# Polynomial sketch attention and a normalised two-layer network on one core: the same calls in another written order, with other PSUM banks

## The chip, the cores and the metric

One Trainium2 chip, one of its cores. The metric is the device time of one execution in microseconds (us), the median of several runs. The engines of a core are TensorE (PE; PEld is its weight load), VectorE (DVE), ScalarE (ACT), GpSimd (POOL) and SyncE (SP), which here only issues DMAs. Each runs its own queue in the written order and waits on semaphores of the others.

## The reference, cut to what matters

```python
def phi(x):                                   # x: (4, 4, 1088, 32), S1, S2: (8, 32)
    a = einsum('rd,bhsd->bhsr', S1, x)
    b = einsum('rd,bhsd->bhsr', S2, x)
    return einsum('bhsi,bhsj->bhsij', a, b).reshape(..., 64)
q_p, k_p = phi(q), phi(k)
kv  = einsum('bhsf,bhsd->bhfd', k_p, v);  z = sum(k_p, axis=2)
x   = einsum('bhsf,bhfd->bhsd', q_p, kv) / (einsum('bhsf,bhf->bhs', q_p, z) + 1e-6)
x   = x.transpose(0, 2, 1, 3).reshape(4, 1088, 128)      # heads side by side
xn  = (x - mean(x)) / sqrt(var(x) + 1e-6) * g_ln         # over the last axis
out = x + maximum(xn @ w_ch1, 0) @ w_ch2                 # (128, 512), (512, 128)
```

Queries, keys, values and the gain are float32; S1, S2 and both weights come as float64, and the kernel puts float32 words together from their halves. All matmuls are float32.

## The kernel before, in words

There are four batches, 0 to 3. The 1088 tokens of a batch and its four heads go through these calls; each call is a small function in the kernel, and its name is used below.

*Words of S, W1 and W2.* `w_ex`, `w_bits`, `w_mant`, `w_e2`, `w_low`, `w_add`, `w_e3` (the sign merge, L310), `w_mul` (L87 by its helper) work with integer and float operations on DVE, ACT and POOL. Index 0 is S, 1 is W1, 2 is W2. `s_heads` ends S (tile s_f), `w_mul 1` gives w1g, and `fold` multiplies it by a centring matrix with the gain, so that W1 already subtracts the mean.

*Keys.* `ld k b` brings the keys of batch b (tile kn, two buffers: batches 0 and 2 share one, 1 and 3 the other). `turn_g` and `turn_r` turn them on DVE (L419, L429), `k_feat` multiplies them by the sketch (L537, tiles of 64x32), `k_tok` turns the result (L546, tile kf), `k_prod` forms the 64 products on POOL (L87, tile kp, one buffer for all batches), `k_val` sums products with values (L587, needs all of V of its batch), `k_vcp`, `k_spr` (L602), `k_rcp` bring the sum into tile kvr. `k_sum` (L561), `k_zs`, `k_sc` (L575) and `k_sccp` make the vector for the denominators; for batch 0 `k_scr`, `gram_d`, `gram_r` do that.

*Values.* `ld_v b g` loads a quarter of V (32 partitions, 128 KB), `ld_vr` a rest of 16 KB. Each batch has a V tile of its own.

*Queries.* Batch 0 is turned by TensorE (`turn_p`, L438, copied by `turn_c`) and multiplied by `q_dir` (L621); the others are turned by DVE, then `q_feat` (L655) and `q_tok` (L664). `q_ac`, `q_den`, `q_rec`, `q_a2`, `q_prod` form denominators and products (DVE and POOL, L87, L677, L684), `q_turn` (L702, L707, L712) turns the products. `num` (L725, tiles of 32x32) multiplies them by kvr; `num_cp` and `num_r` copy the numerators into xT and xTr.

*The network.* Its rows go in chunks: c 0 to 7 are halves of the batches (512 rows, batch c // 2), 8 and 9 hold the remaining rows of two batches each. `row_turn`, `row_wr`, `row_rd` bring a chunk through DRAM into rows (tile x); `st_bn`, `st_ag`, `st_pow` give the reciprocal deviation (tile rstd). `hid z c j t0 t1` (L834) multiplies xT by a quarter j of W1 into PSUM bank z, `relu` copies it into one of two hidden buffers hT (which one goes by the chunk's place in 0, 1, 2, 3, 8, 4, 5, 6, 7, 9), `sec z c t` (L850) multiplies a block of 128 rows by W2 into bank z. `fin` (DVE), or `fin_a` (ACT) and `fin_g` together, scale by rstd and add x; `store` and `store_r` write out.

*Fillers.* `fill n w z` runs n products of ones, w columns wide, into bank z. Their results are not used.

*What sets the order.* Nothing is scheduled by a planner. The string PROGRAM (L901) lists all 498 calls; a loop behind it makes them in that order, so each engine's queue is this list restricted to its calls. A, V, G, S in a call name the engine ACT, DVE, POOL or SP. The numbers z are PSUM banks, chosen by hand: a call that writes a bank waits until the copies out of it are done. An engine stands still behind the first call that waits.

```python
    for line in PROGRAM.split(";"):
        if line.split():
            name, *args = line.split()
            ops[name](*(int(a) if a.isdigit() else a for a in args))
```

## Time and profile before

| | |
|---|---|
| median of 3 runs | 103.19 us (102.77 to 103.45) |
| the profiled execution | 103.05 us, span of its instructions 101.2 us |
| granted TensorE clock | 1.00 throughout |
| read from HBM, written | 9.84 MB, 4.33 MB |
| PE | 95.8 us busy, 1273 matmuls |
| DVE, POOL, ACT | 73.2, 57.9, 38.8 us busy |

An fp32 product shows as two matmuls, a transpose as one. A matmul's end is modelled and lies behind the start of the next one, so distances between starts are the measure of what PE spends. In the DMA rows the last number is the time from issue to landing. In the waits, "issue" stands where the profile shows no releaser.

### The profile page before, as it was taken

What the parts mean: (1) busy time and instruction counts of PE and PEld (TensorE: products, weight loads), DVE (VectorE), ACT (ScalarE), POOL (GpSimd) and SP (SyncE); (2) the same over time, 40 slices, a digit from 0 to 9 for tenths busy, and PEclk for the clock granted to TensorE, in tenths of its full rate; (3) what the DMA queues carried; (4) which work ended last, traced back from release to release, by engine and by line L of the source; (5) the groups of instructions that cost most, each with busy time, mean ns of one, the idle gap of its engine ahead of it and who ended that gap; (6) DMA issues with size and microseconds to landing.
All of it is one profiled execution on the core that took longest, in us unless ns stands there. A gap on an engine that the chain in (4) does not pass through costs nothing.

```text
span 101.2 us, 3143 instructions
## 1 busy us (share of the span) xinstructions
PE 95.8 (95%) x1273; PEld 67.2 (66%) x1273; DVE 73.2 (72%) x213; ACT 38.8 (38%) x92; POOL 57.9 (57%) x80
## 2 busy tenths in 40 slices
PE   4999999999899999999999999999999999999970
PEld 2634777667453989674559794786378966888950
DVE  5397799989697899599998455998939029833440
ACT  3460523237296311253775183065550532133000
POOL 6046998999339979947099990195193400403400
PEclk9999999999999999999999999999999999999999
DMA  2898999999179500025550055700004661200341
GB/s 32 294 361 291 269 218 216 345 279 286 41 233 305 148 15 6 0 84 161 189 158 4 6 207 187 233 1 0 0 6 176 242 197 40 104 0 6 125 170 41
DMA packets 13119, 14.37 MB, mean 142 GB/s; under 512 B 2480, under 2 KB 10160, under 8 KB 13104
## 3 DMA queue, kind: packets, MB, share of 16 engines
q1 hardware_dynamic: 12912, 14.09, 45.8%
q8 instruction: 10, 0.16, 0.7%
q10 hardware_dynamic: 192, 0.07, 0.3%
q14 instruction: 5, 0.04, 0.1%
HBM read 9.84 MB, written 4.33 MB: 140 GB/s over the span
## 4 chain that ended last, share of the span: by engine, by line
PE 94%; DVE 1%; issue 1%; ACT 1%; ACTq 1%
PE ALL L850 31%; PE ALL L834 30%; PE ALL L257 8%; PE ALL L725 7%; PE ALL L587 4%; PE ALL L537 3%; PE ALL L621 2%; PE ALL L655 2%; PE ALL L438 1%; PE ALL L561 1%; PE ALL L602 1%; PE ALL L367 1%; ACTq L894 1%; DVE ones L196 0%; PE ALL L575 0%
## 5 line engine op out<-in xcount | busy, mean ns | idle before, releaser
L850 PEld LDWEIGHTS ALL<-w,hT 128*128 128x128 f32 x272 | 32.2, 192 | 4.8 <-issue 4.0
L850 PE MATMUL ALL<-w,hT 128*128 128x128 f32 x272 | 33.7, 277 | 0.0
L834 PE MATMUL ALL<-xT,w 128*128 128x512 f32 (+1 forms) x72 | 30.7, 552 | 0.0
L842 ACT ACTIVATE hT<-ALL 128x512 f32<-128x512 f32 (+2 forms) x34 | 15.8, 486 | 16.2 <-PE ALL L834 9.3
L834 PEld LDWEIGHTS ALL<-xT,w 128*128 128x128 f32 x72 | 12.3, 190 | 8.0 <-issue 5.0
L87 POOL TENSOR_TENSOR kp<-kf 128x768 f32<-128x768 f32 (+2 forms) x9 | 17.4, 1943 | 0.0
L87 POOL TENSOR_TENSOR qp<-a,fq 128x512 f32<-128x512 f32 (+3 forms) x7 | 13.8, 1979 | 3.2 <-DVE a L87 3.0
L818 POOL TENSOR_TENSOR va<-mv,eps 128x4 f32<-128x4 f32 (+1 forms) x10 | 2.0, 200 | 15.9 <-DVE mv L813 15.9
L868 ACT ACTIVATE ob<-ALL,rstd 128x128 f32<-128x128 f32 x20 | 6.9, 370 | 10.5 <-PE ALL L850 3.8
L257 PE MATMUL ALL<-ones 128*128 128x256 f32 (+1 forms) x18 | 9.3, 642 | 1.5 <-DVE ones L196 1.5
L820 POOL TENSOR_TENSOR rstd<-va,mhalf 128x4 f32<-128x4 f32 (+1 forms) x10 | 9.2, 923 | 2.3 <-DVE ob L863 1.6
L82 ACT COPY xT<-ALL 128x256 f32<-128x256 f32 x10 | 5.8, 648 | 10.2 <-PE ALL L725 8.0
L787 DVE STREAM_TRANSPOSE xh<-ALL 128x256 f32<-128x256 f32 x16 | 6.3, 421 | 4.4 <-issue 2.7
L844 DVE TENSOR_SCALAR hT<-ALL 128x512 f32<-128x512 f32 (+2 forms) x10 | 6.0, 604 | 3.9 <-PE ALL L834 3.9
L725 PE MATMUL ALL<-qpT,kvr 32*32 32x288 f32 (+2 forms) x320 | 7.8, 364 | 0.6 <-issue 0.4
L863 DVE SCALAR_TENSOR_TENSOR ob<-ALL,rstd,x 128x128 f32<-128x128 f32 x12 | 3.7, 343 | 6.1 <-PE ALL L850 5.4
L702 DVE STREAM_TRANSPOSE qpT<-qp 128x1024 f32<-128x1024 f32 (+1 forms) x6 | 8.0, 1348 | 0.0
L807 DVE BATCH_NORM_STATS2 st<-x 128x6 f32<-128x128 f32 x32 | 6.8, 273 | 0.0
L315 POOL TENSOR_TENSOR mant<-mant,low 128x512 f32<-128x512 f32 x2 | 2.5, 1271 | 7.2 <-ACT mant L298 7.2
L725 PEld LDWEIGHTS ALL<-qpT,kvr 32*32 32x32 f32 x320 | 4.1, 103 | 3.6 <-issue 1.0
L257 PEld LDWEIGHTS ALL<-ones 128*128 128x128 f32 x18 | 4.0, 250 | 3.7 <-DVE ones L196 1.5
L664 DVE STREAM_TRANSPOSE fq<-ALL 128x576 f32<-128x576 f32 x6 | 4.3, 763 | 2.6 <-PE ALL L655 2.4
(111 smaller groups left out, 115.6 us busy)
## 6 DMA issues: line engine op xcount, KB each, us to landing
kn<-in_k_dram SPq DMA_DIRECT2D x4, 544.0 KB, 5.9
vn<-in_v_dram SPq DMA_DIRECT2D x16, 128.0 KB, 4.2
xd<-xh SPq DMA_DIRECT2D x8, 256.0 KB, 2.3
x<-xd SPq DMA_DIRECT2D x8, 256.0 KB, 3.7
out_dram<-ob SPq DMA_DIRECT2D x7, 256.0 KB, 2.4
qn<-in_q_dram SPq DMA_DIRECT2D x3, 544.0 KB, 7.0
w_raw<-in_moe_w_ch_dram SPq DMA_DIRECT2D x2, 512.0 KB, 5.7
qt<-in_q_dram SPq DMA_DIRECT2D x1, 512.0 KB, 5.3
```

Source lines behind the costliest of these rows:

```text
L87: by[eng].tensor_tensor(out=o, in0=a, in1=b, op=ALU.mult)
L257: pe.matmul(bank(z, 0, w), ones[:, 0:P], ones[:, 0:w], start=True, stop=True)
L702: dve.transpose(_ap(qpT, 0, P, 32 * u0, [[32, u1 - u0], [TW, 8], [1, 32]]), qp[:, H * F * u0 : H * F * u1])
L725: pe.matmul(bank(z[r], o, o + w)[D * h : D * h + D], kvr[b % 2][rows, DM * f + D * h : DM * f + D * h + D], qpT[rows, c : c + w], start=(f ...
L787: dve.transpose(_ap(xh[slot(c)], 0, P, 64 * n * i, [[32 * n, 2], [32, n], [1, 32]]), pair(z, P * (c % 2), [[32, n], [1, 32]]))
L807: dve.bn_stats(out=sts[slot(c)][:, 6 * t : 6 * t + 6], in_=row_ap(c, t))
L820: pool.tensor_tensor(out=rstds[slot(c)][:, 0:n], in0=vas[slot(c)][:, 0:n], in1=mhalf[:, 0:n], op=ALU.pow)
L834: pe.matmul(bank(z, 0, n), w1[:, P * j : P * (j + 1)], cols(c)[:, a : a + n], start=True, stop=True)
L842: act.activation(o, i, AF.Relu)
L844: by[eng].tensor_scalar(out=o, in0=i, scalar1=0.0, scalar2=None, op0=ALU.max)
L850: pe.matmul(bank(z, DM * t, DM * (t + 1)), h[:, 512 * j + P * t : 512 * j + P * (t + 1)], w2[:, DM * j : DM * (j + 1)], start=(j == 0), st ...
L868: act.activation(ob(c)[:, P * t : P * (t + 1)], bank(z, P * t, P * (t + 1)), AF.Copy, scale=rstds[slot(c)][:, t : t + 1])
```

## The change

The function bodies stay as they are; PROGRAM is another list. It has 498 calls again, of the same kinds: 44 `hid`, 34 `sec`, five `num`, four each of `k_feat` and `k_val`, three 512-wide and six 256-wide `fill`, the same loads and stores. Every engine gets its calls in another order, most PSUM banks differ, and some calls are on another engine: `w_mant 0` on ACT instead of DVE, `w_mul 2` and a net of one `q_a2`, two `q_ac` and one `q_prod` on POOL instead of DVE, a net of three `relu`, two `num_r` and one `num_cp` on DVE instead of ACT.

Of the list, its head:

```diff
-    ld_s A 1; c_iota; c_small; ld_s A 0; c_ones; fill 1 512 7; fill 1 256 5; fill 1 256 4; c_vpad 0;
+    ld_s A 1; c_vpad 0; c_rest; c_small; c_iota; c_pads 0; c_ones; fill 1 256 5; fill 1 512 4; ld_s
...
```

Three places carry the steps of the prediction.

First SP's queue at its start. kn_68 holds batches 0 and 2, kn_69 batches 1 and 3; qt is q of batch 0, vn_74 is V of batch 0, vn_75 V of batch 1, w_raw here is W2.

```order
 L123 DMA kn_68<-in_k_dram 128x1088
+L123 DMA kn_69<-in_k_dram 128x1088
+L146 DMA qt<-in_q_dram 128x4x256
 L155 DMA qt<-in_q_dram 64x4x32
-L146 DMA qt<-in_q_dram 128x4x256
-L123 DMA kn_69<-in_k_dram 128x1088
 L123 DMA kn_68<-in_k_dram 128x1088
-L131 DMA vn_74<-in_v_dram 32x4x256
+L165 DMA w_raw<-in_moe_w_ch_dram 128x4x128
 L137 DMA vn_74<-in_v_dram 32x4x32
-L131 DMA vn_74<-in_v_dram 32x4x256 x2
+L131 DMA vn_74<-in_v_dram 32x4x256 x3
```

Keys 1 now go out ahead of the queries of batch 0; W2 stands directly behind keys 2 and ahead of all of V 0. Before, W2 followed q 1 and parts of V 1 and V 3, ten places later. V of batches 1 to 3 follows later than before relative to the other loads: ahead of most of V 1 stand now k 3 and q 3.

Second PE's queue between the first numerators and the second part of them. kf_133 and skq are keys and sketch of batches 2 and 1, qT_99 the queries of batch 1, xT_149 is chunk 0.

```order
 L575 MATMUL ALL<-zT,s2b 128x32
+L561 MATMUL ALL<-kf_133 32x32 x9
 L725 MATMUL ALL<-qpT,kvr_138 32x128 x32
-L561 MATMUL ALL<-kf_133 32x32 x9
-L257 MATMUL ALL<-ones 128x256
-L834 MATMUL ALL<-xT_149,w_123 128x256 x2
 L655 MATMUL ALL<-qT_99,skq_103 32x288 x16
+L834 MATMUL ALL<-xT_149,w_123 128x256 x5
 L575 MATMUL ALL<-zT,s2b 128x32
-L834 MATMUL ALL<-xT_149,w_123 128x256 x4
 L725 MATMUL ALL<-qpT,kvr_138 32x160 x32
```

`k_sum 2` moved ahead of the first `num`, a fill went (to the head, ahead of `k_feat 0`), and `q_feat 1` stands ahead of all `hid`, of which five instead of six come before the second `num`. Further up, both `fold` moved from beside `k_spr 0` to between `q_dir` and `k_sum 1`, ahead of `k_val 0`.

Third POOL's queue in the middle. kp is the product of keys, qp that of queries, w_124 is W2, ac and a are denominators' terms and scaled sketches, rstd_184 and rstd_183 belong to chunks 1 and 0. Before:

```order
L87 TENSOR_TENSOR kp<-kf_134 128x1280
L87 TENSOR_TENSOR ac_101<-fq 128x16x8
L87 TENSOR_TENSOR ac_101<-fq 128x20x8
L315 TENSOR_TENSOR mant_120<-mant_120,low_121 128x512
L410 COPY skq_104<-skq_103 128x16
L87 TENSOR_TENSOR a_148<-fq,rden_146 128x128
L87 TENSOR_TENSOR qp<-a_148,fq 128x1024
L87 TENSOR_TENSOR a_148<-fq,rden_146 128x160
L87 TENSOR_TENSOR qp<-a_148,fq 128x1280
L818 TENSOR_TENSOR va_180<-mv_177,eps 128x4
L820 TENSOR_TENSOR rstd_183<-va_180,mhalf 128x4
```

And now:

```order
L87 TENSOR_TENSOR kp<-kf_134 128x1280
L87 TENSOR_TENSOR a_148<-fq,rden_146 128x160
L87 TENSOR_TENSOR a_148<-fq,rden_146 128x128
L87 TENSOR_TENSOR qp<-a_148,fq 128x1280
L87 TENSOR_TENSOR qp<-a_148,fq 128x1024
L237 MEMSET vn_76 64x4x32
L87 TENSOR_TENSOR kp<-kf_133 128x1280
L87 TENSOR_TENSOR kp<-kf_133 128x1024
L87 TENSOR_TENSOR ac_100<-fq 128x16x8
L87 TENSOR_TENSOR ac_100<-fq 128x20x8
L818 TENSOR_TENSOR va_181<-mv_178,eps 128x4
L820 TENSOR_TENSOR rstd_184<-va_181,mhalf 128x4
```

W2's addition and its product w_124 now stand above the first row shown; below it, both products of batch 2's keys come ahead of the first rstd, and chunk 1's comes ahead of chunk 0's. In ACT's queue `fin_a 4 1 0`, which needs that rstd, stands directly ahead of `num_cp A 1 1 4 8`, `k_vcp 2`, `num_cp A 1 0 4 8` and `fin_a 5 1 3`; before, the first `fin_a` of chunk 1 came behind all copies of that `num`.

On PE the groups `k_feat 3`, `k_val 1`, `q_feat 2` now follow each other, as do `num 1`, `k_sum 3`, `k_val 2`. On DVE the two operations `w_bits 1` and `w_ex 1` stand between the operations on S, `k_zs 0` behind `turn_g k 1`, and `w_e3 2` behind `q_tok 1`. At the end the last `sec` is that of chunk 9 in both lists; `fin 4 7 1` now stands between it and the last `fin`. `c_act`, a single ACT operation on one column, moved from the end of the list to the first `hid`.

## The prediction

> **What bounds the kernel now.** I read the page first: busy shares, then the chain that ended last.

> ```profile
> PE 95.8 (95%) x1273; PEld 67.2 (66%) x1273; DVE 73.2 (72%) x213; ACT 38.8 (38%) x92; POOL 57.9 (57%) x80
> PE 94%; DVE 1%; issue 1%; ACT 1%; ACTq 1%
> ```

> TensorE is busy 95% of the span and is 94% of the chain. The change removes no operation, so time can only come from places where PE waits, where it changes shape, or from the two ends. Next I read who PE waited for; these are its two longest:

> ```profile
> PE ALL L257 <- DVE ones L196: 1.5, 1, 1.5
> PE ALL L725 <- issue: 0.4, 1, 0.4
> ```

> The 1.5 is the start and stays. The ends of matmuls are modelled, so part of a wait hides behind them; the starts are measured. I therefore read PE's timeline by its starts (start, length, what), up to where the network part begins:

> ```profile
> 8.73 0.72 PE L537 MATMUL ALL<-kT,sk 64*32 64x288 f32 x16
> 9.37 1.13 PE L257 MATMUL ALL<-ones 128*128 128x512 f32 x2
> 10.43 0.38 PE L561 MATMUL ALL<-kf 128*32 128x32 f32 x18
> 12.12 1.10 PE L621 MATMUL ALL<-skd,qT 128*128 128x96 f32 x8
> 15.97 1.21 PE L587 MATMUL ALL<-kp,vn 128*32 128x64 f32 x72
> 19.37 1.44 PE L725 MATMUL ALL<-qpT,kvr 32*32 32x128 f32 x64 [0.22 <-ACT w L82]
> 21.72 1.10 PE L834 MATMUL ALL<-xT,w 128*128 128x256 f32 x4
> 22.75 0.77 PE L655 MATMUL ALL<-qT,skq 32*32 32x288 f32 x32
> 23.45 0.41 PE L575 MATMUL ALL<-zT,s2b 128*128 128x32 f32 x2
> 25.60 0.46 PE L725 MATMUL ALL<-qpT,kvr 32*32 32x160 f32 x4
> 26.42 1.14 PE L725 MATMUL ALL<-qpT,kvr 32*32 32x160 f32 x60 [0.37 <-issue]
> 27.50 4.57 PE L834 MATMUL ALL<-xT,w 128*128 128x256 f32 x12
> ```

> What a group costs is the distance to the next start. Behind 27.50 I find no further wait, only a price for changing between full tiles and tiles of 32 rows or columns. In the chain of waits three `sec` stand once between two tiled groups and once between full ones:

> ```profile
> 57.03 2.87 PE ALL L850 x24
> 79.11 2.68 PE ALL L850 x24
> ```

> Two borders cost 0.19 us, about 0.1 each.

> **Term 1, the head up to the first `hid`.** S goes through DVE, then the keys are turned, and POOL multiplies (two of the three products of batch 0 in the last row):

> ```profile
> 6.09 0.41 DVE L87 TENSOR_TENSOR s_f<-mant,ex 8x256 f32<-8x256 f32 x1
> 6.62 1.25 DVE L419 STREAM_TRANSPOSE kT<-kn 128x1024 f32<-128x1024 f32 x1
> 11.81 1.23 DVE L419 STREAM_TRANSPOSE kT<-kn 128x1024 f32<-128x1024 f32 x1
> 10.65 2.97 POOL L87 TENSOR_TENSOR kp<-kf 128x768 f32<-128x768 f32 x2
> ```

> The change puts two operations on W1's words (some 0.4 each) among those on S, where one stood before, and sends one operation on S round by ACT: s_f ends near 7.05 instead of 6.50, the turn near 8.4, the sketch near 8.55. PE has one fill more in that time, and `k_feat 0` starts at 8.7 as before. Behind it now stand two fills, one as in the row at 9.37 (1.06 to the next start, its wait included) and one half as wide (0.5): `k_sum 0` starts near 10.85 instead of 10.43. `k_zs` now stands behind the 1.23 turn of batch 1's keys and ends near 11.6; `k_scr`, the query turns and `gram_d` behind it put `q_dir 0 4` at 12.45 instead of 12.12. From `q_dir` to `k_val 0` PE took 3.85; the same groups stand there now and the two folds with them (two 256-wide matmuls, 0.9): `k_val 0` at 17.2. POOL's three products are ready near 15.3 (from 10.8, 1.5 each). `num` started 3.40 behind `k_val`; the folds (0.9) leave that stretch, the wait of 0.22 for the second one's copy goes too, `k_sum 2` (0.38) comes in: `num` at 19.85. `q_feat 1` waits for the turn of q 1 on DVE, which the order lets start near 19.8 and which takes 1.2 and a small one: 21.2. It runs 0.7, and `hid` stands behind DVE's copy of the numerators: 22.2. Before, `hid` began at 21.72 with `q_feat` (22.75 to 23.45) still to do, as good as 22.42. Term 1: **-0.2**, between -0.7 (PE free of the 0.4 that the fills hold it up) and +1.6 (V late, below).

> **Term 2, the wait inside `num 0 4 9`.** Four matmuls start at 25.60 and sixty at 26.42. The whole took 1.90; sixty took 1.08, so 64 without the hole take some 1.25. They wait for DVE's turn of the products that POOL makes last. In the new order POOL has them near 21.7, DVE has turned them by 24.4, and PE arrives at 24.6. **-0.65**; at worst 0, if DVE is later than PE by as much as now.

> **Term 3, borders.** From the first `hid` to the end the old order has nine runs of tiled groups. The new one sets `k_feat 3, k_val 1, q_feat 2` and `num 1, k_sum 3, k_val 2` side by side and does `q_feat 1` before the first `hid`: six and a half. 2.5 x 0.19 is **-0.5**, between -0.3 and -0.6.

> **Term 4, new waits.** POOL gets W2's last product, and by its order has no pause for sixteen us behind it. The product needs DVE's sign merge (last two rows, W1's and W2's):

> ```profile
> 9.08 1.26 POOL L87 TENSOR_TENSOR w1g<-mant,ex 128x512 f32<-128x512 f32 x1 [0.81 <-DVE ex L310]
> 25.23 0.93 POOL L87 TENSOR_TENSOR ac<-fq 128x128 f32<-128x128 f32 x2
> 31.89 2.29 POOL L87 TENSOR_TENSOR qp<-a,fq 128x1024 f32<-128x1024 f32 x1
> 34.67 2.40 POOL L87 TENSOR_TENSOR qp<-a,fq 128x1280 f32<-128x1280 f32 x1
> 39.11 1.95 POOL L87 TENSOR_TENSOR kp<-kf 128x1024 f32<-128x1024 f32 x1
> 38.10 1.03 POOL L820 TENSOR_TENSOR rstd<-va,mhalf 128x4 f32<-128x4 f32 x1
> 8.24 0.68 DVE L310 SCALAR_TENSOR_TENSOR ex<-w_raw,e 128x512 uint32<-128x512 uint32 x1
> 30.26 1.13 DVE L310 SCALAR_TENSOR_TENSOR ex<-w_raw,e 128x512 uint32<-128x512 uint32 x1
> ```

> The merge follows DVE's turns and a `q_tok` and ends near 26.0. From there POOL owes 1.26 (W2), 0.93 (`q_ac 1`), 2.40 (`k_prod 1 0 5`, as wide as the row at 34.67), 0.93 (`q_a2 1`), 2.40, 2.29, 2.40, 1.95 (`q_prod 1`, `k_prod 2`), 0.93 (`q_ac 2`) and 1.25 (`st_pow 1`): 16.7, with small overlaps 16.5, so `rstd` of chunk 1 comes at 42.5. `fin_a 4 1 0` on ACT waits for it, and behind it are queued two `num_cp`, `k_vcp` and `fin_a 5 1 3`, of such lengths:

> ```profile
> 42.84 0.36 ACT L868 ACTIVATE ob<-ALL,rstd 128x128 f32<-128x128 f32 x1
> 44.27 0.62 ACT L82 COPY xT<-ALL 128x256 f32<-128x256 f32 x1
> ```

> That ends near 44.8, and `hid 5 3 0`, which needs the copy and the bank, would be PE's turn at 44.5: 0.3. Two closer meetings, `hid 2 3 3` behind the relu of its bank and `num 3` behind DVE's `q_turn 4 9`, get 0.25 more as an estimate. **+0.55**, between 0 and +1.4.

> The tail stays: in both orders the last `sec` is followed by one `fin` on DVE and a store on two queues. `c_act` leaves the end of ACT's queue and costs ACT some 0.2 near 22.5, where it has room before its next relu.

> ```profile
> 97.67 0.35 DVE L863 SCALAR_TENSOR_TENSOR ob<-ALL,rstd,xr 128x128 f32<-128x128 f32 x1 [0.47 <-PE ALL L850]
> ```

> Sum: -0.2 - 0.65 - 0.5 + 0.55 = **-0.8 us**. The profiled execution took 103.05 (its span 101.2 and 1.85 around it), so 102.25 for its like. The median shown, 103.19, lies 0.14 above it, and I forecast **102.4**.

> **Rivals.** *V of batch 0 is late: slower.* W2 now goes out behind the keys of batch 2 and ahead of V of batch 0. Issue (start) and landing (last number, us from the issue) of W2, of keys 3 behind it and of the last part of V 0:

> ```profile
> 13.79 0.43 SPq L165 DMA_DIRECT2D w_raw<-in_moe_w_ch_dram  x1
> w_raw<-in_moe_w_ch_dram SPq DMA_DIRECT2D x1, 512.0 KB, 7.8
> 14.46 0.35 SPq L123 DMA_DIRECT2D kn<-in_k_dram  x1
> kn<-in_k_dram SPq DMA_DIRECT2D x1, 544.0 KB, 9.0
> 10.77 0.43 SPq L131 DMA_DIRECT2D vn<-in_v_dram  x1
> vn<-in_v_dram SPq DMA_DIRECT2D x1, 128.0 KB, 4.7
> ```

> Keys 3 landed at 23.46, W2 at 21.59: in a full queue such a load takes 1.87. V was there at 15.47; 1.87 later is 17.3, and up to 0.8 less because keys 1 and the queries now follow each other with no pause of the queue: 16.5 to 17.3, against 17.2 where `k_val 0` asks. From 18.0 on the lateness eats the whole gain. At 19.0, as if W2 cost twice that, all PE work behind it moves by 1.8 and the time is 102.4 + 1.8 = 104.2. Against it: the range I find ends at 17.3. [...]

> *POOL sets the pace: no change.* If its unbroken line ends 0.8 later, `hid 5 3 0` waits 1.1, and the time is 103.2. For it: the merge took 1.13 in one case and 0.68 in the other, and POOL's product waits for it. Against it: the durations in the sum were taken beside a busy DVE already.

> ```profile
> 29.57 1.27 POOL L315 TENSOR_TENSOR mant<-mant,low 128x512 f32<-128x512 f32 x1 [3.40 <-ACT mant L298]
> ```

> [...]

> *None of the new waits comes: faster.* Term 4 is 0, the time 101.85. For it: each meeting is missed by tenths only. Against it: there are three.

> *The early loads bring nothing.* W2 landed at 21.59, long before PE was through chunk 1's `hid` (27.50 and 4.57); earlier is no gain in itself. If the order gives no more than that, the time is the even one, 103.2.

> **How the numbers follow.** The forecast (101.9 to 102.9) has 0.46, no new wait 0.22, the two even cases together 0.17, V late 0.15. One per cent, 1.03 us, is about what a measurement of this kernel can tell from no change. Below 102.16 lie the 0.22 and a third of the forecast: faster 0.37. Above 104.22 lies most of V late, since once late it is late by whole loads: slower 0.12. Within: 0.51. The range 101.5 to 103.9 leaves out the best fifth of the fast case and most of V late, 0.17 together.

> **What would show it.** Right: first `hid` near 22.2 with `q_feat 1` done; `num 0 4 9` in one piece; `k_val 0` with no wait; a late start of some 0.3 at `hid 5 3 0`, when ACT stands behind `rstd`. Wrong: PE idle before L587 with a V load as releaser; `rstd` of chunk 1 after 43.5; a late start of more than 0.5 beyond 45; a tail of more than 3.6 behind the last `sec`.

## The result and the profile after

The new order takes 102.19 us (median of four executions, 101.63 to 103.61); the old one, beside it, 103.32. The ratio is 0.9899, with a 95% interval of 0.9854 to 0.9943: about 1% faster. The forecast was 102.4. The ratios here leave out executions that ran long, most of them at a lower granted clock; where those are the subject themselves, the text says so.

The profiled execution took 101.63, its span is 99.9: 1.38 less than before (99.857 against 101.233). The page first, TensorE's share and the chain, then who TensorE waited for:

```profile
PE 94.1 (94%) x1273; PEld 67.0 (67%) x1273; DVE 71.7 (72%) x213; ACT 37.4 (37%) x87; POOL 61.3 (61%) x85
PE 80%; DVE 10%; DMA 4%; issue 2%; ACTq 1%; ACT 0%; DVEq 0%
```

```profile
PE ALL L367 <- DVE kT L429: 0.5, 1, 0.5
PE ALL L834 <- DVE xT L84: 0.2, 1, 0.2
PE ALL L655 <- DVE zT L569: 0.2, 1, 0.2
```

The old wait "issue" at L725 is gone. DVE now has a tenth of the chain: TensorE arrives at the network a little ahead of it. TensorE's timeline by its starts, to be laid beside the one of before:

```profile
8.43 0.72 PE L537 MATMUL ALL<-kT,sk 64*32 64x288 f32 x16
10.56 0.38 PE L561 MATMUL ALL<-kf 128*32 128x32 f32 x18
12.38 1.03 PE L621 MATMUL ALL<-skd,qT 128*128 128x96 f32 x8
17.12 1.21 PE L587 MATMUL ALL<-kp,vn 128*32 128x64 f32 x72
19.81 1.06 PE L725 MATMUL ALL<-qpT,kvr 32*32 32x128 f32 x64
21.04 0.85 PE L655 MATMUL ALL<-qT,skq 32*32 32x288 f32 x32 [0.17 <-DVE zT L569]
22.13 2.76 PE L834 MATMUL ALL<-xT,w 128*128 128x256 f32 x10 [0.24 <-DVE xT L84]
24.97 1.17 PE L725 MATMUL ALL<-qpT,kvr 32*32 32x160 f32 x64
26.07 1.13 PE L834 MATMUL ALL<-xT,w 128*128 128x256 f32 x4
```

The first `hid` starts at 22.13 with `q_feat 1` done (22.2 was forecast), and the second numerators are one piece of 1.10 (24.97 to 26.07) where 1.90 stood. From the first `hid` to the end, all distances between TensorE's starts but those of `q_feat` and of these numerators sum to 0.30 less than before. So the 1.38 consists of:

| term | forecast | measured |
|---|---|---|
| 1, head up to the first `hid` (22.42 before, `q_feat` counted) | -0.2 | -0.29 |
| 2, inside `num 0 4 9` | -0.65 | -0.80 |
| 3 and 4, borders and new waits | -0.5 + 0.55 | -0.30 |

Of the head's 0.29, 0.15 is in the first numerators (1.23 to the next start; 1.38 before). These 1.38 are of two single executions; the medians differ by 1.13, and the interval of the ratio allows 0.6 to 1.5. What term 4 rested on, POOL's reciprocal deviation of chunk 1, then ACT behind it, then TensorE, is in these rows of three engines:

```profile
41.59 1.04 POOL L820 TENSOR_TENSOR rstd<-va,mhalf 128x4 f32<-128x4 f32 x1
```

```profile
42.67 0.37 ACT L868 ACTIVATE ob<-ALL,rstd 128x128 f32<-128x128 f32 x1 [4.70 <-POOL rstd L820]
44.05 0.38 ACT L868 ACTIVATE ob<-ALL,rstd 128x128 f32<-128x128 f32 x1
```

```profile
43.09 0.33 PE L777 MATMUL ALL<-ident,xTr 128*128 128x128 f32 x1
44.59 0.59 PE L834 MATMUL ALL<-xT,w 128*128 128x512 f32 x1
```

POOL ends at 42.63 (42.5 forecast). ACT is through with `fin_a 5 1 3` at 44.43, not 44.8: its operations start 0.26 to 0.41 apart, less than their durations (0.37 to 0.64), which I had added up. `hid 5 3 0` at 44.59 is not late. The tail is 3.6 in both.

### The profile page after: what moved, and what is told of

It reads as the page before. It is cut to its first block, busy times and chain, and to the rows that moved or that the text cites. A ratio compares the mean times of both kernels' runs of the same rounds, so it can differ in the third digit from the quotient of the medians.

```text
span 99.9 us, 3146 instructions
## 1 busy us (share of the span) xinstructions
PE 94.1 (94%) x1273; PEld 67.0 (67%) x1273; DVE 71.7 (72%) x213; ACT 37.4 (37%) x87; POOL 61.3 (61%) x85
## 4 chain that ended last, share of the span: by engine, by line
PE 80%; DVE 10%; DMA 4%; issue 2%; ACTq 1%; ACT 0%; DVEq 0%
PE ALL L850 31%; PE ALL L834 29%; PE ALL L725 6%; DMA s_raw<-in_S_dram 4%; PE ALL L587 3%; PE ALL L257 2%; PE ALL L537 2%; DVE kf L546 2%; PE ALL L655 1%; PE ALL L438 1%; DVE qpT L707 1%; DVE qT L419 1%; PE ALL L621 1%; DVE fq L664 1%; PE ALL L602 1%
## 5 line engine op out<-in xcount | busy, mean ns | idle before, releaser
L850 PEld LDWEIGHTS ALL<-w,hT 128*128 128x128 f32 x272 | 32.4, 192 | 5.2 <-issue 4.5
L850 PE MATMUL ALL<-w,hT 128*128 128x128 f32 x272 | 33.4, 276 | 0.0
L834 PE MATMUL ALL<-xT,w 128*128 128x512 f32 (+1 forms) x72 | 30.7, 551 | 0.3 <-DVE xT L84 0.2
L842 ACT ACTIVATE hT<-ALL 128x512 f32<-128x512 f32 (+2 forms) x31 | 15.3, 498 | 16.6 <-PE ALL L834 14.2
L834 PEld LDWEIGHTS ALL<-xT,w 128*128 128x128 f32 x72 | 12.2, 190 | 8.2 <-issue 3.5
L87 POOL TENSOR_TENSOR kp<-kf 128x768 f32<-128x768 f32 (+2 forms) x9 | 17.4, 1942 | 0.1
L87 POOL TENSOR_TENSOR qp<-a,fq 128x1024 f32<-128x1024 f32 (+3 forms) x8 | 14.7, 1842 | 2.0 <-DVE a L87 1.7
L868 ACT ACTIVATE ob<-ALL,rstd 128x128 f32<-128x128 f32 x20 | 6.8, 370 | 13.6 <-POOL rstd L820 8.0
L844 DVE TENSOR_SCALAR hT<-ALL 128x512 f32<-128x512 f32 (+2 forms) x13 | 7.3, 565 | 4.9 <-PE ALL L834 4.1
L702 DVE STREAM_TRANSPOSE qpT<-qp 128x1280 f32<-128x1280 f32 (+1 forms) x6 | 8.2, 1370 | 3.0 <-POOL qp L87 3.0
L257 PE MATMUL ALL<-ones 128*128 128x256 f32 (+1 forms) x18 | 8.6, 611 | 1.5 <-DVE ones L196 1.5
L820 POOL TENSOR_TENSOR rstd<-va,mhalf 128x4 f32<-128x4 f32 (+1 forms) x10 | 9.2, 923 | 0.8
L863 DVE SCALAR_TENSOR_TENSOR ob<-ALL,rstd,x 128x128 f32<-128x128 f32 x12 | 3.9, 347 | 5.4 <-PE ALL L850 4.9
L725 PE MATMUL ALL<-qpT,kvr 32*32 32x288 f32 (+2 forms) x320 | 7.0, 364 | 0.1
L257 PEld LDWEIGHTS ALL<-ones 128*128 128x128 f32 x18 | 4.0, 246 | 4.5 <-issue 2.5
L82 ACT COPY xT<-ALL 128x256 f32<-128x256 f32 x9 | 5.5, 641 | 3.8 <-PE ALL L725 2.7
L725 PEld LDWEIGHTS ALL<-qpT,kvr 32*32 32x32 f32 x320 | 3.9, 103 | 2.1 <-DVE st L807 0.8
L587 PEld LDWEIGHTS ALL<-kp,vn 128*32 128x32 f32 x288 | 4.2, 110 | 1.4 <-issue 1.4
## 6 DMA issues: line engine op xcount, KB each, us to landing
kn<-in_k_dram SPq DMA_DIRECT2D x4, 544.0 KB, 6.4
vn<-in_v_dram SPq DMA_DIRECT2D x16, 128.0 KB, 4.9
qn<-in_q_dram SPq DMA_DIRECT2D x3, 544.0 KB, 4.6
w_raw<-in_moe_w_ch_dram SPq DMA_DIRECT2D x2, 512.0 KB, 4.5
qt<-in_q_dram SPq DMA_DIRECT2D x1, 512.0 KB, 7.5
```

Of the source, the lines that this page charges most:

```text
L87: by[eng].tensor_tensor(out=o, in0=a, in1=b, op=ALU.mult)
L257: pe.matmul(bank(z, 0, w), ones[:, 0:P], ones[:, 0:w], start=True, stop=True)
L587: pe.matmul(bank(z, 0, F)[D * h : D * h + D], vn[b][:, TW * h + D * u : TW * h + D * (u + 1)], kp[:, F * m : F * (m + 1)], start=(u == 0), ...
L702: dve.transpose(_ap(qpT, 0, P, 32 * u0, [[32, u1 - u0], [TW, 8], [1, 32]]), qp[:, H * F * u0 : H * F * u1])
L725: pe.matmul(bank(z[r], o, o + w)[D * h : D * h + D], kvr[b % 2][rows, DM * f + D * h : DM * f + D * h + D], qpT[rows, c : c + w], start=(f ...
L820: pool.tensor_tensor(out=rstds[slot(c)][:, 0:n], in0=vas[slot(c)][:, 0:n], in1=mhalf[:, 0:n], op=ALU.pow)
```

## The experiments

All ratios are to the old order on the same chip.

**What the hole in `num 0 4 9` was.** Term 2 had the size, but I went back to its cause. The prediction said that the sixty products wait for DVE's turn of the products. This is the last such turn in the old order:

```profile
22.51 1.20 DVE L707 STREAM_TRANSPOSE qpT<-qp 128x1024 f32<-128x1024 f32 x1
```

It ended at 23.71, the numerators began at 25.60 and stopped after four matmuls: it can't be that. The program has no semaphore wait at the fifth matmul either. Something else fits. Both pages have a queue that the profile calls "instruction":

```profile
q8 instruction: 10, 0.16, 0.7%
```

These are ten transfers of 16 KB, called blocks below. In the old order's DMA records the second one runs from 24.03 to 25.16, and TensorE goes on at 26.42; in the new order it runs from 21.36 to 22.31. The stretches around it, one row per us, for the old and the new order (the last two columns are the share of the DMA engines, which passes 1 where the records of transfers overlap, and GB/s):

```profile
20.00:21.00 1.00, 1.00 (x76) 0.74 (x54) 0.61 (x3) 0.28 (x1) 1.00 (x2) 1.00 1.19 345
21.00:22.00 1.00, 1.00 (x16) 0.61 (x5) 1.00 (x3) 0.34 (x1) 1.00 (x1) 1.00 1.08 250
```

```profile
20.00:21.00 1.00, 0.87 (x64) 0.54 (x44) 1.00 (x3) 0.07 (x1) 1.00 (x2) 1.00 0.04 17
21.00:22.00 1.00, 0.85 (x32) 0.34 (x32) 0.99 (x3) 1.00 (x3) 1.00 (x2) 1.00 0.06 16
```

The old order keeps the DMA engines full up to 24.9. In the new one SP's queue stands at the load of queries 3 from 15.2 to 21.1, and they run empty from 20 to 22. The new theory: TensorE waits for its instructions, and these wait for the loads. The test holds loads back in the old order and touches nothing else (on SP):

```diff
-ld_v S 3 2; ... ld_v S 2 1; ... ld_v S 1 0; row_wr S 0; ld_v S 1 1; ... ld_v S 1 3; ... row_rd S 0;
+row_wr S 0; ... row_rd S 0; ld_v S 1 0; ld_v S 1 1; ld_v S 1 3; ld_v S 2 1; ld_v S 3 2;
```

> The old order with five loads of 128 KB (three quarters of V 1, one each of V 2 and V 3) taken from SP's queue where they stand and put behind the first read of rows; no engine's own order changes. In the trace of the old order the hole of 0.65 us inside the second numerators stands before their third product, which waits for no semaphore, while the DMA engines are full up to 24.9 us and a block of 16 KB on the instruction queue is moved at 24.03 to 25.16; in the new order that block is moved at 21.36 to 22.31 and the DMA engines are idle at 20 to 21. Theory (TensorE waits for its instructions, which wait behind the loads): with 0.64 MB less ahead of it the queue is empty by about 23, the block comes earlier, the hole shrinks from 0.65 to 0.2 or less, and the time falls by about 0.6 us against the old order. Rival (the prediction's: the hole is DVE's turn of the products): DVE's queue is as before, the hole stays at 0.65 and the time at that of the old order, within 0.2 us.

Measured: 101.84 (101.84 to 101.91), ratio 0.9881 (0.9843 to 0.9919). TensorE's rows there, its queue the same as in the old order to the last instruction:

```profile
19.21 1.22 PE L725 MATMUL ALL<-qpT,kvr 32*32 32x128 f32 x64 [0.23 <-ACT w L82]
25.21 1.18 PE L725 MATMUL ALL<-qpT,kvr 32*32 32x160 f32 x64
26.32 1.99 PE L834 MATMUL ALL<-xT,w 128*128 128x256 f32 x6
```

```profile
21.00:22.00 1.00, 1.00 (x5) 0.64 (x4) 1.00 (x5) 0.00 (x0) 1.00 (x1) 1.00 0.20 65
```

The hole is gone, and a smaller one that I had not told apart in the first numerators has shrunk (1.16 to the next start, 1.38 before). The block moved at 21.46 to 22.55, as the engines ran empty. Of the 1.17 by which the span is shorter, 0.80 is the hole, 0.22 the smaller one, and the rest lies in the head, ahead of both. Five loads moved give as much as the new order, whose 1.38 has 0.95 at the same two places; DVE's turn is out as the cause.

Next, whether the hole stands at an instruction rather than at a datum. In the old order 16 more instructions go ahead of it:

```diff
-num_cp A 0 0 0 4 6 7; k_sccp V 1 3; fill 1 256 3;
+num_cp A 0 0 0 4 6 7; k_sccp V 1 3; fill 5 48 3;
```

> The old order with the filler ahead of the first product of the network written as five narrow products (48 columns) in place of one of 256: about as much time, 16 more instructions on TensorE ahead of the second numerators. Theory (the hole stands at a boundary of instruction blocks): it moves 16 instructions towards the start, so no longer inside the second numerators but at one of the two products of the network ahead of them, with a length of 0.4 to 1.5 us there, and the numerators run in one piece of 1.1. Rival (a wait for data of the numerators): the hole stays where it was, four matmuls behind their start, at 0.65. Time within 0.3 us of the old order by both.

Measured: 104.24, ratio 1.0121 (1.0069 to 1.0174). The numerators run in one piece, and a pause now stands at the same count of loads of weights in another group, inside `hid`, as the theory had it:

```profile
25.56 0.73 PEld L834 LDWEIGHTS ALL<-xT,w 128*128 128x128 f32 x4
26.48 0.73 PEld L834 LDWEIGHTS ALL<-xT,w 128*128 128x128 f32 x4 [0.18 <-issue]
```

The last load of the first row starts at 26.10 and the next one 0.37 later, where 0.22 is usual there. This was shorter than expected, and the matmuls, a load behind, did not feel it: TensorE came there late, 1.07 behind the block's landing. The expected equal time was wrong. The ten narrow matmuls took 1.18 where the two wide ones took 0.67, and in the profile the granted clock was 0.50 from 22.04 to 25.45; but two executions at full clock were as slow (104.21, 104.69), so the clock is not all of it. More was learned from all traces together. I counted TensorE's loads of weights from 0 and looked for pauses between two of them, inside a group, with no wait behind them (the count is that of the last load before the pause):

| kernel | block moved | last load before, next load | count | behind the landing |
|---|---|---|---|---|
| old order | 17.07 to 18.46 | 19.41, 19.81 | 219 | 1.34 |
| old order | 24.03 to 25.16 | 25.63, 26.42 | 346 | 1.26 |
| narrow fillers | 16.87 to 18.24 | 19.05, 19.68 | 219 | 1.44 |
| narrow fillers | 23.93 to 25.03 | 26.10, 26.48 | 346 | 1.44 |
| loads held back | 16.02 to 17.44 | 19.25, 19.43 | 219 | 1.99 |
| loads pushed, new order (below) | 21.20 to 22.58 | 22.94, 24.14 | 220 | 1.56 |
| groups parted (below) | 42.41 to 43.40 | 43.89, 44.80 | 727 | 1.40 |
| loads pushed, old order (below) | 17.28 to 18.61 | 19.73, 20.07 | 219 | 1.45 |
| loads pushed, old order (below) | 23.84 to 25.44 | 25.88, 26.68 | 346 | 1.24 |

The counts differ by 127 or a multiple of it, give or take one (727 is 346 and 3 x 127), and 127 pairs of a load and a matmul are 254 instructions. In these rows TensorE goes on 1.24 to 1.56 behind the landing, whatever group stands there; only the row of the loads held back, a pause of 0.18, lies further behind (1.99). Where the block had landed 1.88 or more ahead of that load (2.69 at load 346 in the new order), no trace has a pause. That the blocks hold TensorE's next instructions is my theory, from the name of the queue, these counts and these distances; what is in a block no trace shows. All but one of the pauses stand in tiled groups, where 127 pairs can last as little as 2.4 us (load 600 at 40.18, load 727 at 42.55 in the new order).

The reverse, in the new order: loads pushed ahead of the one at which SP stands.

```diff
-ld S k 3 0 34; num_cp A 0 1 0 4 3 4; ld S q 3 0 34;
+ld S k 3 0 34; num_cp A 0 1 0 4 3 4; ld_v S 1 0; ld_v S 3 3; ld_v S 1 2; ld_v S 1 1; ld_v S 3 2; ld_v S 2 3; ld_v S 2 2; ld_v S 3 0; ld S q 3 0 34;
```

> The new order with eight loads of 128 KB of V 1, V 2 and V 3 put ahead of the load of the queries of batch 3, at which SP's queue stands from 15.2 to 21.1 us; no engine's own order changes. They fill the DMA engines in the stretch 19 to 23 us that is empty now. Theory (instructions behind loads): the block of 16 KB that now moves at 21.36 to 22.31 comes up to a microsecond later and slower, TensorE stands 0.3 to 1.0 us near the start of the second numerators (now 24.97), and the new order loses that much: 102.5 to 103.2 where the new order has 102.2. Rival (the hole was DVE's): no engine waits for these loads earlier than now, the time is that of the new order within 0.2 us.

Measured: 103.62, ratio 1.0003 (0.9956 to 1.0049): the gain was gone, and the profile has a pause at the first of these counts (load 220), in another group:

```profile
22.90 0.26 PE L561 MATMUL ALL<-kf 128*32 128x32 f32 x5
24.14 0.32 PE L561 MATMUL ALL<-kf 128*32 128x32 f32 x13 [0.98 <-issue]
```

But in that profile the clock was 0.50 from 7.83 to 14.66 and TensorE came 3.5 us late into the stretch, so loads and clock were mixed. The five executions at full clock took 102.60 to 103.11, so most of the loss went with the clock. The push was run again with a filler that keeps the clock up (its diff stands in the next part):

> The order with the eight loads pushed ahead, and the same filler. In the profile of the order without the filler TensorE stood 1.2 us at its 220th weight load, inside another group than before but at the same count, 1.56 after the first block of 16 KB had landed (22.58). Theory (instructions behind loads): the hole is there again at the 222nd weight load (two more in the filler), 1.3 to 1.5 after the landing, and the order is 0.8 to 1.5 us slower than the one with the filler alone. Rival (what it lost was the clock alone): it is within 0.3 of the one with the filler alone.

Measured: 102.01, ratio 0.9887 (0.9842 to 0.9933), with no pause, and no slower than the order with the filler alone (0.9896). I expected 0.8 to 1.5 above, and that was wrong; by its time the rival holds, that the clock alone had cost what was lost. The second block did come later (22.03 to 23.36; 19.70 to 20.90 with the filler alone), with the DMA engines full, but its load comes at 25.25, 1.89 behind the landing. So it is not shown that the new order owes its gain to SP's stand: it stays without a pause when eight loads fill that time. The old order with more loads ahead:

```diff
-ld S k 3 0 34;
+ld S k 3 0 34; ld_v S 1 1; ld_v S 1 3; ld_v S 2 0;
```

> The old order with three loads of 128 KB (two of V 1, one of V 2) put forward on SP's queue, directly behind the keys of batch 3: the opposite of the run that held five loads back. No engine's own order changes. So far every stop of TensorE that waits for no semaphore (0.40 and 0.79 between two loads of weights in the old order, 1.20 and 0.90 in two variants of the new) stood at its weight load 219 or 346 or 727 (one more or less), that is at multiples of 127 further on, and 1.26 to 1.56 behind the landing of a block of 16 KB. Theory (blocks of instructions behind loads): 0.38 MB more at about 0.3 MB a us delays block one from 24.03 to 25.16 by 0.6 to 1.3, so the stop at load 346 grows from 0.65 to 1.2 to 1.9, the one at load 219 is 0.2 to 1.2, and the time is 0.6 to 2.0 us above the old order. Rival (in the run with loads held back something else than the blocks got faster): the stop stays at 0.65, the time within 0.3 of the old order.

Measured: ratio 1.0007 (0.9958 to 1.0057). The same two pauses, no longer:

```profile
25.85 0.46 PE L725 MATMUL ALL<-qpT,kvr 32*32 32x160 f32 x4
26.68 1.14 PE L725 MATMUL ALL<-qpT,kvr 32*32 32x160 f32 x60 [0.37 <-issue]
```

I expected the stop at load 346 to grow to between 1.2 and 1.9, and that was wrong: in number this is what the rival expected, that something other than the blocks had got faster with the loads held back. Against the rival stand the counts and the distances from the landings, which fit the table. The engines were full there already and stayed full (a share of 1.12 to 1.22 from 21 to 24), and the block's delay did not grow with the bytes put ahead of it, as it did in the run before. When a block is asked for is not in the trace: that stays open.

**The clock.** In two variants the granted clock fell to 0.50 in the head (from 7.83 to 14.66 in the one with loads pushed; the one with V of batch 0 late, below, had a mean of 0.977), and one execution of the new order had a mean clock of 0.983. The order itself, and one with one more filler product ahead of the sketch:

```diff
-w_addlow V 0 0 64; fill 1 256 5;
+w_addlow V 0 0 64; fill 2 256 5;
```

> The new order as it is, beside the three that follow. The four kernels run so far showed that a stretch of 3.41 us in which TensorE was busy 0.67 or less is followed by one or more at half the clock, and that the new order has TensorE idle ahead of the sketch while it waits for S (0.48 us in its own profile, 1.13 and 1.82 in the two variants of it). Theory: with S as late as there, executions of the new order fall into two groups, near 101.7 and, with one such stretch in the head, 1.2 to 1.7 higher. Rival (the clock's drop came of the changed loads): all runs lie within 0.5 of 102.0.

> The new order with one more filler (256 wide) ahead of the sketch, so that TensorE's idle time while it waits for S shrinks by 0.43 us at the full clock. Theory (the idle time there costs the clock): no stretch at half the clock in the head, and the median comes to 101.6 to 101.9, with the spread of its runs under 0.5. Rival (the filler is only work added ahead of the path): 0 to 0.4 us slower than the new order as it is.

Measured, the order itself: ratio 0.9891 (0.9834 to 0.9948) and, by single executions, 101.75, 102.23, 102.66 and then 104.06, 104.19, 105.61, the last three with a mean clock of 0.98, 0.983 and 0.966. With the filler: 0.9896 (0.9855 to 0.9937), all six between 101.80 and 102.77 with a clock of 0.996 to 1.0. Half the clock lasted 3.41 (22.04 to 25.45 with the narrow fillers, 10.33 to 13.74 in the order itself) or twice that (7.83 to 14.66 with loads pushed). Stretches of that length, as the clock's records cut them (PE's busy time first, the clock third from the end), of the order itself and of the filler:

```profile
6.92:10.33 3.41, 2.33 (x26) 1.39 (x26) 2.31 (x6) 0.65 (x2) 1.69 (x3) 1.00 0.66 232
10.33:13.74 3.41, 3.41 (x24) 1.66 (x25) 2.19 (x5) 0.27 (x1) 3.41 (x4) 0.50 0.95 314
```

```profile
4.37:7.78 3.41, 2.45 (x13) 1.55 (x11) 2.58 (x9) 2.47 (x5) 0.78 (x1) 1.00 0.93 351
7.78:11.20 3.42, 3.42 (x44) 1.73 (x44) 3.42 (x9) 0.44 (x2) 3.42 (x5) 1.00 0.88 287
```

Here busy 0.68 of a stretch of 3.41 was followed by half the clock, and busy 0.72 was not. That is no threshold, though the expectation has one: the drop in the run with narrow fillers came behind a stretch of 0.86, and in the mixed variant below, stretches counted on from its clock's records, one of 0.57 is followed by none:

```profile
21.20:24.61 3.41, 1.95 (x36) 1.02 (x36) 3.41 (x5) 1.68 (x4) 2.59 (x2) 1.00 0.65 200
24.61:28.03 3.42, 3.21 (x74) 2.62 (x75) 3.31 (x6) 2.99 (x8) 2.56 (x5) 1.00 0.93 231
```

The two groups of executions came, the upper one further up than expected; the filler's median (102.29 against 103.36 over all six) missed its 101.6 to 101.9. That the filler keeps the clock up is borne out by all variants of the new order together: without it 18 of 33 executions had a mean clock below 0.99, with it 2 of 44. How idle TensorE must be for the clock to fall these runs do not tell. In undisturbed executions the filler brings nothing (0.9896 against 0.9891).

**V of batch 0 late.** The rival of the prediction, brought about:

```diff
-ld_w S 2 0 4; ... ld S q 1 0 34;
+ld_w S 2 0 4; ld S q 1 0 34;
```

> The new order with the queries of batch 1 (544 KB) put ahead of V of batch 0, directly behind W2. The last part of V 0 is issued at 11.51 and lands 4.8 later, at 16.3, and the product that needs it starts at 17.12: a margin of 0.8. The prediction's rival had a load of this size cost what follows it 1.87. If that price holds, V 0 lands at 18.2, TensorE waits 1.1 for it and all behind it moves by 0.6 to 1.1: 102.8 to 103.3. If loads issued by one queue share the engines so that order matters little, V 0 lands within 0.8 of now and the time stays at 102.2.

Measured: 103.59, ratio 1.0028 (0.9987 to 1.0069).

```profile
19.09 1.11 PE L587 MATMUL ALL<-kp,vn 128*32 128x64 f32 x65 [0.25 <-issue]
```

V's loads took 7.0 us where 4.8 to 5.1 stood, 2.0 more: the prediction's price of 1.87 was near. TensorE waited only 0.25 in this profile, since a stretch at half the clock had made it 1.6 late already (`q_dir` at 14.03). The five executions at full clock took 102.45 to 103.77; what they waited for was not profiled. The new order's own margin is 0.8 (issue at 11.51, landing 16.3, use at 17.12), against the 0 that the rival's upper end gave it.

**Borders.** In the order with the filler, `sec` and `hid` put between the tiled groups that stand side by side:

```diff
+sec 7 1 1;
 k_val 1 0 9 0;
+sec 7 1 2;
 q_feat 2 3 5 2 6;
...
-sec 7 1 1; ... sec 1 1 2;
...
+hid 2 8 3 0 1;
 k_val 3 0 9 0;
...
-hid 2 8 3 0 1;
```

The second of the two `sec` changes its bank from 1 to 7, and the `fin_a` that reads it comes earlier than before.

> The new order with the filler ahead of the sketch, and its side-by-side tiled groups parted: one block of chunk 1 (into bank 7) stands between the keys of batch 3 and the product with values of batch 1, one between that and the queries of batch 2, and the product of the remaining rows between the queries of batch 3 and the last product with values. The operations are the same. That makes three more pairs of borders between full tiles and tiles of 32 rows or columns. Theory (two borders cost 0.19 us): the distances between TensorE's starts grow by 0.57 in sum at these places, and the end comes that much later than with the filler alone. By what the whole change measured behind the first product of the network (0.30 for 2.5 pairs) it is 0.36. Rival (borders cost nothing, the 0.30 came from elsewhere): 0 to 0.1.

Measured: 104.51, ratio 1.0119 (1.0056 to 1.0181).

```profile
32.22 0.72 PE L537 MATMUL ALL<-kT,sk 64*32 64x288 f32 x16
32.86 1.16 PE L850 MATMUL ALL<-w,hT 128*128 128x128 f32 x8
33.95 1.21 PE L587 MATMUL ALL<-kp,vn 128*32 128x64 f32 x72
35.09 1.16 PE L850 MATMUL ALL<-w,hT 128*128 128x128 f32 x8
36.18 0.77 PE L655 MATMUL ALL<-qT,skq 32*32 32x288 f32 x32
...
41.53 1.59 PE L725 MATMUL ALL<-qpT,kvr 32*32 32x288 f32 x64 [0.59 <-DVE qT L429]
43.29 0.87 PE L587 MATMUL ALL<-kp,vn 128*32 128x64 f32 x46
44.79 0.61 PE L587 MATMUL ALL<-kp,vn 128*32 128x64 f32 x26 [0.63 <-issue]
```

A `sec` between two tiled groups takes 1.09 (32.86 to 33.95, and 35.09 to 36.18), between full ones 0.89: 0.20 for two borders, as forecast from the old order. Most of the rest of the loss is new: a wait for DVE of 0.59, and behind it a pause of 0.9 at load 727. There the DMA engines were idle (share 0.00 from 40 to 42), so this block came late without loads in its way. TensorE had stood until 41.53, just ahead of load 600, the count 127 before it, and the block moved only from 42.41; that this wait held the block up is likely, but one trace does not show it.

**POOL's line (term 4).** The two reciprocal deviations exchanged, in the order with the filler:

```diff
-st_ag 1; st_pow 1; ... st_bn 0; st_ag 0; ... st_pow 0;
+st_ag 1; st_bn 0; st_ag 0; st_pow 0; st_pow 1;
```

> The new order with the filler ahead of the sketch, and the two reciprocal deviations of chunks 0 and 1 on POOL in the other order, so that chunk 1's comes 1.30 us later (its power ended at 42.63, the next one takes 1.30). Theory (the prediction's term 4 named the right chain, and only its 0.3 was wrong: the first product of chunk 3 in bank 5 started at 44.59, 0.16 behind the end of ACT's copy out of that bank at 44.43): that product now starts late by 1.1 to 1.3 and all behind it moves, so the time is 1.1 to 1.3 above the order with the filler alone. Rival (the chain does not bind, ACT's order leaves room): TensorE waits less than 0.3 there.

Measured: 103.87, ratio 1.0089 (1.0044 to 1.0134).

```profile
42.78 1.21 PE L587 MATMUL ALL<-kp,vn 128*32 128x64 f32 x72
45.86 0.33 PE L777 MATMUL ALL<-ident,xTr 128*128 128x128 f32 x1 [1.87 <-ACT ob L868]
```

The chain is real, but its first victim is `row_pe 8 4`, which writes the bank that `fin_a 4 1 0` reads: 43.09 behind 43.04 in the new order, a margin of 0.05. The prediction named `hid 5 3 0`, further on. The shift was 1.9 and not 1.3, since POOL also waited 0.6 for DVE's sums of chunk 0.

**A better head.** DVE has no pause from 14.2 to 22.0 in the new order. The mixed variant (the filler, and the changes its expectation lists; in it one block of rows of chunk 1 is scaled out of a bank that has been written again, so its output differs there, with the same amount of work):

```diff
-q_ac V 0 0 4; w_bits V 2 0 512; ... ld_vr S 0 1; w_ex V 2 0 512;
+num_cp V 0 0 0 4 0 1; w_bits V 2 0 512; ... q_turnr; w_ex V 2 0 512;
...
-k_sum 0 2; turn_g k 1 0 4; ... k_zs 0 2; k_scr 5; gram_d 5; gram_r 5;
+k_sum 0 2; ... k_zs 0 2; k_scr 5; gram_d 5; gram_r 5; turn_g k 1 0 4;
```

> The new order with the filler ahead of the sketch; in its head the turn of batch 1's keys on DVE stands behind the two parts of the sketch for the denominators, the 512-wide filler ahead of the first sum of keys is a 256-wide one, and the 256-wide one behind the first product with values is 128 wide; DVE's two operations on the words of W2 are moved out of the stretch from 15 to 16 us behind the first numerators and the turns of the products, W2's product on POOL goes behind the two denominators' terms of batch 1, and the first output of chunk 1 behind the second. Theory (in the new order DVE, without a pause from 14.2 to 22.0, sets when the network begins; 0.8 of it is W2's words): the first product of the network starts 0.5 to 0.8 earlier than in the order with the filler alone, and the time falls by 0.4 to 0.8 against it. Rival (POOL's line sets the middle, the gain is given back at the first products of chunk 3): the start is earlier but the time the same within 0.2.

Measured: 103.54, ratio 1.0027 (0.9999 to 1.0055). The first `hid` came 0.50 earlier, counted from the sketch, but the time rose by 1.3 against the order with the filler alone, which neither theory nor rival had. DVE and POOL there, and DVE's same operation in the new order:

```profile
22.07 2.00 DVE L288 TENSOR_SCALAR bits<-w_raw 128x512 uint32<-128x512 uint32 x1
```

```profile
21.84 1.94 POOL L87 TENSOR_TENSOR kp<-kf 128x1024 f32<-128x1024 f32 x1
```

```profile
15.15 0.41 DVE L288 TENSOR_SCALAR bits<-w_raw 128x512 uint32<-128x512 uint32 x1
```

Beside POOL's product the operation took 2.00 and ended 0.29 behind it; alone 0.41. The new order has it where POOL pauses (15.08 to 16.79). A turn of DVE of 128x1024 took 1.20 in the old order with POOL busy throughout (the row at 22.51 above) and 1.24 with POOL idle (at 70.64). What made the operation longer no row shows. With W2's operations back in place, the filler, the second part of that diff, and two fillers narrower:

```diff
-k_tok 0 2 5; fill 1 512 6;
+k_tok 0 2 5; fill 1 256 6;
...
-fill 1 256 2;
+fill 1 128 2;
```

> The order with the filler ahead of the sketch, and of the mixed variant before only the head: the turn of batch 1's keys on DVE behind the two parts of the sketch for the denominators, a 256-wide filler for the 512-wide one ahead of the first sum of keys, 128 for 256 behind the first product with values. W2's two operations on DVE stay where the new order has them. In the mixed variant, which had them beside a product of POOL's, the first of them took 2.00 us (22.07 to 24.07; 0.41 in the new order, where POOL pauses), ended 0.3 behind POOL's product, and TensorE waited 1.36 for the transposition behind it; from the sketch to the first product of the network it took 14.66, against 15.16 with the filler alone. Theory: without that meeting the 0.4 to 0.5 of the head stays, the time is 0.4 to 0.5 below the order with the filler alone, 101.5 to 101.9, faster than both kernels. Rival (what the head gains is given back at the first products of chunk 3, behind POOL's line): the same time within 0.15.

Measured: 102.04 (101.85 to 102.23), ratio 0.9889 (0.9846 to 0.9932): no faster than the filler alone (0.9896) beyond the interval. From the sketch to the first `hid` 14.95 us passed instead of 15.16, not 14.66, and the 0.2 is gone at the end (92.8 from sketch to end against 92.9). No version was measured to be faster than the new order by more than its interval; the old order with five loads held back reaches it.

## Why the prediction was right, and where not

- *The verdict* was right: 102.19 against 102.4. The sum (0.8) fell short of the 1.38 of the profiled executions by 0.58 and of the 1.13 of the medians by 0.33. As to the cause of its largest term it was luck (term 2).
- *Term 1* was right, step by step (10.56 for 10.85, 12.38 for 12.45, 17.12 for 17.2, 19.81 for 19.85, 22.13 for 22.2). Two errors cancel in it: `k_feat 0` started at 8.43, not 8.7, and from `k_sum 0` to `q_dir` 1.82 passed, not 1.60.
- *Term 2* had the place and nearly the size (0.65; 0.80 measured) by the wrong cause. "They wait for DVE's turn" fell to a row of the old profile, where that turn ends 1.9 ahead, and to the run with five loads held back, in which the hole vanishes with DVE's and TensorE's queues untouched. "Issue" in the waits had said that no releaser was known; I put the nearest suspect there. The rival "the early loads bring nothing" asked what the loads bring by landing early. Holding later ones back brings the most in the old order. In the new one the block lands 2.69 ahead of its load; that SP's stand from 15.2 to 21.1 is what it takes was not borne out, as eight loads in that time cost nothing once the clock was kept up.
- *Term 3* had the right price, 0.20 for two borders in the run with the groups parted.
- *Term 4* was the mis-sized term: 0.55 at three meetings behind 26 us, and none cost anything. The chain was real (1.9 in the run with the deviations exchanged), with 0.05 and 0.16 to spare. It came earlier than I had it because ACT's operations overlap. In its place there is one wait that I had not seen: the third `hid` starts 0.26 late behind DVE's `q_tok 1` (its predecessor takes 0.69 to the next start instead of 0.43). With it, terms 3 and 4 together gave -0.30 instead of +0.05.
- *POOL sets the pace* did not come: W2's merge took 0.66 (25.32 to 25.98), with POOL pausing from 24.97 to 26.13; in the old order it took 1.13, with POOL at work.
- *V late* had the right price for a load and too little margin; of the three waits of term 4 none came, as *none of the new waits* had it; another one did.

## What to carry to other kernels

Where the waits show "issue" inside a dense group of small matmuls, look when the instruction blocks moved and whether the loads filled the DMA engines then; loads that nobody needs for ten us may be better issued behind that place (in the old order five of them gave the whole gain). Count what a wait is worth only after checking the end of the thing it is said to wait for. A row of operations that overlap is measured from start to start, also on ACT (0.26 to 0.41 apart here, at durations of 0.37 to 0.64).
